# A prompt kernel whose mixer moves out of attention into a stage of its own

## The chip, the core and the metric

One core of a Trainium2 chip. The metric is the device time of one execution in microseconds, less is better. TensorE (PE) does matrix products, with its weight loads shown as PEld; VectorE (DVE), ScalarE (ACT) and GpSimd (POOL) do the rest; SyncE (SP), ACT and GpSimd issue DMAs, each through a queue that it works off in order.

## The reference

2048 tokens of width 576; 32 query heads on 16 key heads of width 128; attention sees the last 512 keys for every query, without a mask.

```
def _A_ref(x, k_cache, v_cache, wq, wo):
    W = min(4096, max(256, Sk // 4))
    q = (x @ wq).reshape(B, Sq, Hq, Dh), as heads
    k = jnp.repeat(k_cache[:, :, Sk - W:, :], rep, axis=1)
    v = jnp.repeat(v_cache[:, :, Sk - W:, :], rep, axis=1)
    p = _softmax(q k^T * (Dh ** -0.5))
    return (p v, heads side by side) @ wo

def _B_ref(x, w1, w2, w3, w4):
    h = _gelu(_layernorm(x, axis=-1) @ w1)
    c = D // 4
    g0, g1, g2, g3 = the four quarters of h, shifted along the tokens by +1, -1, +2, -2
    hs = jnp.concatenate([g0, g1, g2, g3], axis=-1) @ w2
    x1 = x + hs
    h2 = _gelu(_layernorm(x1, axis=-1) @ w3) @ w4
    return x1 + h2

x = A_x
xn = _layernorm(x, axis=-1)
s = _A_ref(xn, A_k_cache, A_v_cache, A_wq, A_wo)
g = _silu(_B_ref(xn, B_w1, B_w2, B_w3, B_w4))
return x + s * g
```

The products with w1 (576 x 576) and w2 (576 x 576), with the shift between them, are the mixer. Those with w3 (576 x 4608) and w4 are the MLP, which the text calls the up and the down product.

## The kernel before

The tokens are worked in 4 blocks of 512 (NB, QB), each of 4 tiles of 128 (TB). 576 is 4 chunks of 128 rows and one of 64 (NF = 4 full, NDC = 5), and on the output side 512 columns and 64 (M0, R0).

**Attention** runs over units u = 32 x block + head, 128 in all (U). A unit computes qT (`stage_q`), four score products with exp (`stage_s`), the value products (`stage_v`: 16 matmuls, a reciprocal and a product on DVE) and the transpose of the head's output into oT by a DMA on SP's queue (`stage_t`). The order of PE's, SP's and GpSimd's instructions is the program's. Other work is hung into the units by two tables: `at(u, fn)` for steps of any engine and `pe(u, atoms)` for matmuls, which are dealt out between the unit's own stages. The output projection of a block (`wo_atoms`: four groups of 32 matmuls of 512 columns, one for each tile, and a last group of 128 with 64 columns) goes into the first units of the next block; that of the last block follows after unit 127, one group after another. The mixer goes the same way: the second layernorm `ln2_steps`, its transposes `tr2`, the first product `b1` (five pieces a block, the last one the 64 remaining columns), its GELU out of tanh and DVE arithmetic (`gelu1`), the shift `b2_shift` of the remainder, and the second product `b2` and `b2_rem`, whose sum x1 goes to DRAM and is read back by `load_x1`.

**The flag.** `finish_flag` reduces the softmax's row sums, sends them through DRAM (`mx_dram`) onto one partition, and computes a flag that takes a safe path at the end where it is set. Its GpSimd part waits in `late`: a copy of one element of the first evicted projection tile into `gate`, ahead of the store.

**The MLP** starts when the last projection ends. Its products run as pairs of matmuls on 64 rows each, one on partitions 0 to 63 (LO) and one on 64 to 127 (HI), which work at the same time and write different banks. `up` does two chunks of 128 hidden columns in 9 such pairs: a first round, a DVE instruction that reads both banks (`fence`), and a second round with the halves crossed. `down` interleaves pairs of 512 and of 64 columns. Weights come in 9 slices (w3_s, w3r_s, w4_s; 4 + 0.5 + 4.5 KB a partition) by SP's queue into memory that attention has left; in the pools of this part each tile waits for the tiles that lay in its place (`reuse_waits="tile"`).

Of the kernel before, what the change touches and what calls it, by code (L numbers as in the profile page):

```python
# [31 lines left out]
def kernel(  # L32
# [45 lines left out]
    HW = OFF + QB + 4  # L78
    B1_ORDER = (4, 0, 1, 2, 3)
# [15 lines left out]
    x1_dram = dram.tile([S, D], BF16, name="x1_dram")  # L95
# [6 lines left out]
    def rsqrt_newton(pool, var, n):  # L102
# [5 lines left out]
        for _ in range(3):  # L108
# [3 lines left out]
            y2 = pool.tile([P, n], FP32, name="nr_y")  # L112
# [76 lines left out]
    xn_b = [keep.tile([P, TB, DP], BF16, name=f"xn_b{i}") for i in range(2)]  # L189
    xnn_b = keep.tile([P, TB, DP], BF16, name="xnn_b")  # L190
    x1_pool = ctx.enter_context(tc.tile_pool(name="x1_pool", bufs=2))
    small = ctx.enter_context(tc.tile_pool(name="small", bufs=4))
    x1_t = {}
    last_t = [None]
    xm_b = [xnn_b, xn_b[0]]
    g_last = xnn_b[:, 0, 0:D]

    def load_x1(b):
        x1 = x1_pool.tile([P, TB, D], BF16, name="x1")
        nc.sync.dma_start(out=x1[:], in_=rows(x1_dram, b * TB, TB))  # L200
        x1_t[b] = x1

    def ln3_steps(b):
        xm = xm_b[b % 2]
        dsts, srcs = [xm[:, tt, :] for tt in range(TB)], [x1_t[b][:, tt, :] for tt in range(TB)]
        return layernorm_small_steps(small, dsts, srcs) if b else layernorm_steps(small, dsts, srcs, twice=True)

    def ln3_transpose(b):
        for tt in range(TB):
            nc.sync.dma_start(out=xT_b[b % 2][:, :, tt * P:(tt + 1) * P], in_=xm_b[b % 2][:, tt, :], transpose=True)  # L210

    with ExitStack() as actx:
# [10 lines left out]
        xnnT = res.tile([P, NDC, QB], BF16, name="xnnT")  # L223
        w1_sb = res.tile([P, NDC, D], BF16, name="w1_sb")
        h4 = res.tile([P, TB, 4, 32], BF16, name="h4")
        w2_sb = res.tile([P, 5, D], BF16, name="w2_sb")
# [9 lines left out]
        hb_pool = pool("hb_pool", 2)  # L236
        hs_pool = pool("hs_pool", 1)
        g1_pool = pool("g1_pool", 1)
        oT_pool = pool("oT_pool", 36)
        wo_sb = pool("a_wo", 1).tile([P, Hq, D], BF16, name="wo_sb")  # L240
# [9 lines left out]
        def x_tile(b):  # L250
            if b < 2:
                xt = hb_pool.tile([P, 5, HW], BF16, name="hb")[:].rearrange("p a b -> p (a b)")
            else:
# [72 lines left out]
        for w in (xn_b[0], xnn_b):  # L326
            nc.gpsimd.memset(w[:, :, D:], 0.0)
# [1007 lines left out]
```

## Time and profile before

| | us |
|---|---|
| median of 3 runs | 821.14 (820.99 to 821.42) |
| span of the profiled execution, first to last instruction | 819.6 |
| PE busy | 810.0 |
| DVE, ACT, GpSimd busy | 467.2, 456.1, 96.4 |
| first matmul of the MLP | 534.85 after the span's start |

For the profiled execution the span is the time on record; the median of the runs lies 1.5 us above it. In a row of a view by line, the line is that of the source, then come the engine, the operation, output and inputs, the count, the busy time and the mean in ns of one, and the idle time in front of it with what ended it. A row of a view by stretches has the stretch, its length, busy time and count for PE, PEld, DVE, ACT and POOL, PE's granted clock, the share of time in which DMA engines were busy, and GB/s. A row of the order of time has start, duration, engine, line and operation. A row of the DMA issues ends with the size and the median us from issue to landing.

### The profile page before, as it was taken

How to read it: one execution, taken by the hardware profiler on the slowest of the kernel's cores; microseconds unless marked ns; L12 is line 12 of the kernel's file. 1: busy time of each engine (PE TensorE's matmuls, PEld its weight loads, DVE VectorE, ACT ScalarE, POOL GpSimd, SP SyncE). 2: the span in 40 equal slices, each digit the busy share in tenths (PEclk: the TensorE clock that was granted, in tenths of full speed). 3: DMA queues.
4: the chain of work that ended last, by engine and by line, in shares of the span. 5: the costliest groups of instructions: out<-in, count | busy, mean ns of one | idle time of the engine just before them, and what ended most of it. 6: DMA issues, size and time to landing. Idle time of an engine off the chain costs nothing. (4 is left out here: it accounts for less than half of the span.)

```text
span 819.6 us, 19524 instructions
## 1 busy us (share of the span) xinstructions
PE 810.0 (99%) x7945; PEld 469.1 (57%) x8031; DVE 467.2 (57%) x1447; ACT 456.1 (56%) x821; POOL 96.4 (12%) x164
## 2 busy tenths in 40 slices
PE   9999999999999999999999999999999999999998
PEld 6666655655564565565465655455555555555555
DVE  6878645678874357964346774044246636655413
ACT  7888853588783368994457983133332433334621
POOL 3443313010100110110001100000000000000000
PEclk9999999999999999999999999999999999999999
DMA  7998983364492144673035553994001221130101
GB/s 197 193 195 197 200 151 81 84 129 76 105 145 58 43 98 120 136 142 57 13 85 121 108 109 97 294 298 101 2 2 44 65 72 45 42 96 16 45 15 38
DMA packets 144156, 84.29 MB, mean 103 GB/s; under 512 B 110128, under 2 KB 136944, under 8 KB 144064
## 3 DMA queue, kind: packets, MB, share of 16 engines
q1 hardware_dynamic: 133408, 53.61, 32.1%
q0 software_dynamic: 9408, 28.15, 13.3%
q8 instruction: 63, 1.03, 0.5%
q10 hardware_dynamic: 1248, 1.25, 0.5%
q14 instruction: 29, 0.24, 0.1%
HBM read 49.17 MB, written 9.29 MB: 71 GB/s over the span
## 5 line engine op out<-in xcount | busy, mean ns | idle before, releaser
L496 ACT ACTIVATE pT<-sc 128x512 bf16<-128x512 f32 x512 | 285.5, 598 | 99.8 <-PE sc L492 90.4
L492 PE MATMUL sc<-qT,kT 128*128 128x512 bf16 x495 | 165.8, 379 | 0.2
L511 PEld LDWEIGHTS <-pT 128*128 128x128 bf16 x2048 | 134.3, 98 | 54.5 <-issue 11.0
L511 PE MATMUL po<-v_sb,pT 128*128 128x129 bf16 x2048 | 158.1, 220 | 0.9
L471 PE MATMUL psq<-xT_b,wq_b 128*128 128x512 bf16 x469 | 125.5, 379 | 1.9
L964 PE MATMUL ph<-xT_b,w_s 64*128 64x512 bf16 x976 | 127.3, 376 | 0.0
L1001 PE MATMUL pm<-w_s,h 64*128 64x512 bf16 x864 | 122.1, 377 | 0.0
L535 PE MATMUL pswo<-wo_sb,oT 128*128 128x512 bf16 x499 | 114.9, 379 | 0.6
L982 ACT ACTIVATE h<-ph 128x512 bf16<-128x512 f32 x67 | 39.4, 597 | 130.6 <-PE ph L964 128.4
L516 DVE TENSOR_TENSOR o<-po,ri_b 128x256 bf16<-128x256 f32 x256 | 107.9, 421 | 6.4 <-DVE ri_b L515 0.3
L1001 PEld LDWEIGHTS <-h 64*128 64x128 bf16 x1728 | 70.6, 94 | 55.4
L535 PEld LDWEIGHTS <-oT 128*128 128x128 bf16 x1024 | 65.2, 98 | 56.5
L1001 PE MATMUL pr<-w_s,h 64*128 64x64 bf16 x864 | 89.9, 189 | 0.0
L964 PEld LDWEIGHTS <-w_s 64*128 64x128 bf16 x1152 | 55.8, 94 | 48.2 <-issue 0.2
L471 PEld LDWEIGHTS <-wq_b 128*128 128x128 bf16 x506 | 49.4, 98 | 57.3 <-issue 1.0
L980 DVE COPY hx<-ph 128x512 f32<-128x512 f32 x55 | 38.1, 692 | 60.3 <-PE ph L964 60.3
L515 DVE RECIPROCAL ri_b<-po 128x2 f32<-128x2 f32 x256 | 42.2, 165 | 48.6 <-PE po L511 44.6
L492 PEld LDWEIGHTS <-kT 128*128 128x128 bf16 x512 | 46.8, 98 | 25.3 <-issue 0.2
L270 POOL DMA_DIRECT2D wq_b<-in_A_wq_dram x30 | 23.3, 776 | 303.8 <-PE sc L492 303.8
L479 DVE TENSOR_TENSOR qT<-psq,rq 128x512 bf16<-128x512 f32 x62 | 42.7, 689 | 27.0 <-ACT pT L496 20.3
L481 DVE CAST qT<-psq 128x512 bf16<-128x512 f32 x40 | 27.6, 689 | 32.9 <-PE psq L456 29.6
L982 ACT ACTIVATE h<-hx 128x512 bf16<-128x512 f32 x55 | 34.6, 630 | 6.0 <-DVE hx L980 1.7
(161 smaller groups left out, 722.7 us busy)
## 6 DMA issues: line engine op xcount, KB each, us to landing
wq_b<-in_A_wq_dram POOLq DMA_DIRECT2D x30, 512.0 KB, 5.1
wo_sb<-in_A_wo_dram POOLq DMA_DIRECT2D x8, 576.0 KB, 5.3
w_s<-in_B_w_dram SPq DMA_DIRECT2D x9, 512.0 KB, 6.8
w_s<-in_B_w_dram SPq DMA_DIRECT2D x10, 288.0 KB, 5.4
x_dram<-x SPq DMA_DIRECT2D x4, 576.0 KB, 4.1
x<-x_dram SPq DMA_DIRECT2D x4, 576.0 KB, 4.1
w_s<-in_B_w_dram SPq DMA_DIRECT2D x4, 576.0 KB, 8.3
s_b<-s_dram SPq DMA_DIRECT2D x4, 576.0 KB, 6.2
```

The lines of the kernel that those rows point to most:

```text
L471: nc.tensor.matmul(psq[:, :], lhsT=w[:, kc, hh * Dh:(hh + 1) * Dh], rhs=xT_b[qb % 2][:, kc, :], start=(kc == 0 and not (two and hh == 1)), ...
L479: behind["qT"] = nc.vector.tensor_tensor(out=qT[:, :], in0=psq[:, :], in1=rq_t.pop(u)[:, :], op=ALU.add)
L492: nc.tensor.matmul(sc[:, :], lhsT=kT[:, g, kc * P:(kc + 1) * P], rhs=qT_t[u][:, :], start=True, stop=True)
L496: behind["exp"] = nc.scalar.activation(out=pT[:, :], in_=sc[:, :], func=ACT.Exp, scale=SCALE)
L511: nc.tensor.matmul(po[:, j, :], lhsT=pTs[kc][:, tt * P:(tt + 1) * P], rhs=v_sb[:, g, kc, 0:Dh + 1], start=(kc == 0), stop=(kc == KCH - 1))
L515: nc.vector.reciprocal(out=ri, in_=po[:, :, Dh])
L516: nc.vector.tensor_tensor(out=o[:, t0:t0 + 2, :], in0=po[:, :, 0:Dh], in1=ri.unsqueeze(2).to_broadcast([P, 2, Dh]), op=ALU.mult)
L535: nc.tensor.matmul(ps, lhsT=oT_t[qb * Hq + h][:, tt, :], rhs=wo_sb[:, h, lo:hi], start=(h == 0), stop=(h == Hq - 1))
L964: nc.tensor.matmul(ps[i][:, :], lhsT=lhsT, rhs=xT[half, kc, :], start=first, stop=last, skip_group_check=True)
L980: nc.vector.tensor_copy(out=src[:, :], in_=ps[i][:, :])
L982: nc.scalar.activation(out=h3[:, :], in_=src[:, :], func=ACT.Gelu_apprx_tanh)
L1001: nc.tensor.matmul(out, lhsT=h3_t[b, fc][half, tt * P:(tt + 1) * P], rhs=w4_s[fc // WS][half, fc % WS, lo:hi], start=key not in started, s ...
```

## The change

The mixer's products, transposes, GELU and shift leave attention's tables. In attention stay the statistics of the second layernorm (`ln2_stats_steps`), and, in the last units, its application for blocks 0 and 1 (`ln2_apply`). xn is kept for all blocks, and x1 is formed in its place, so that `load_x1` and its DRAM copy go. Of the last block's projection, groups 0 and 1 begin within units 127 and 128; then comes the mixer of all four blocks; then groups 2, the small one and 3, and beside them the third layernorm of block 0.

In the stage, `chunk_pair` does two chunks of 512 columns as 9 pairs of 64-row matmuls with a fence between the rounds, as the MLP's `up` does, and `small_products` does the 64-column rest of a block as 18 pairs into two banks, which DVE adds. Each step's first round is issued ahead of the second round of the step before. GELU is one ACT instruction in place of tanh with DVE's arithmetic. The remainder of a block (`b1_rest`) is transposed by a DMA on SP's queue into hq; its shifted copy hs is written by DVE for 64 rows, from hq of the block and of the next one, and by a DMA on SP's queue for the other half. w1 and w2 are loaded at the stage's start by GpSimd's queue, behind `flag_rows`, into memory that attention held; xnnT of all blocks lies there too.

wo_sb, oT and the last projection's staging tile lie at the right edge of the memory. The MLP's weights take that place, `w3_s[0]` and `w3r_s[0]` lying just beside it, and are loaded by GpSimd's queue. In attention, the copies of qT that ACT did in blocks 1 to 3 are DVE's.

```diff
+    xn_b = [keep.tile([P, TB, DP], BF16, name=f"xn_b{i}") for i in range(NB)]
+    xm_b = [keep.tile([P, TB, DP], BF16, name=f"xm_b{i}") for i in range(2)]
+    ln2_mv = [keep.tile([P, TB, 2], FP32, name=f"ln2_mv{i}") for i in range(NB)]
+    ln2_r = [keep.tile([P, TB], FP32, name=f"ln2_r{i}") for i in range(NB)]
...
+    octx = ctx.enter_context(ExitStack())
+    so_last = octx.enter_context(tc.tile_pool(name="so_last", bufs=1, side="right")).tile([P, TB, D], BF16, name="so_last")
+    wo_sb = octx.enter_context(tc.tile_pool(name="a_wo", bufs=1, side="right")).tile([P, Hq, D], BF16, name="wo_sb")
+    oT_pool = octx.enter_context(tc.tile_pool(name="oT_pool", bufs=36, side="right"))
...
-                elif qb == 0 or hh == 0:
+                else:
                     nc.vector.tensor_copy(out=qT[:, :], in_=psq[:, :])
-                else:
-                    nc.scalar.activation(out=qT[:, :], in_=psq[:, :], func=ACT.Copy)
...
+        for b in range(2):
+            for tt in range(TB):
+                at(U - 6 + 2 * b + tt // 2, lambda b=b, tt=tt: ln2_apply(b, tt))
+        wo_last = wo_atoms(NB - 1)[0:2]
+        wo_last = wo_last[0][0:Hq - 1] + wo_last[1][0:8] + [wo_last[0][Hq - 1], flag_rows] + wo_last[1][8:]
+        pe(U - 1, wo_last[0:10])
+        pe(U, wo_last[10:22])
+        pe(U + 1, wo_last[22:])
...
-                c0, c1, c2 = (0, 2, n) if n == 5 else (0, n // 3, 2 * n // 3)
-                if u >= U - 2:
-                    c0, c1, c2 = (0, 5, 5) if u == U - 2 else (2, 4, 4)
+                c0, c1, c2 = (n // 2, n // 2, 3 * n // 4) if u == U else (0, n // 3, 2 * n // 3)
...
+        mctx = ExitStack()
+        mres = pool("m_res", 1, at=mctx)
+        xnnT = [mres.tile([P, NDC, QB], BF16, name=f"xnnT{b}") for b in range(NB)]
...
+        def chunk_pair(ps, lhs, rest_first):
+            n0, n1 = (NDC, NF) if rest_first else (NF, NDC)
+
+            def mm(i, half, k, first, last):
+                lhsT, rhs = lhs(i, half, k)
+                nc.tensor.matmul(ps[i][:, :], lhsT=lhsT, rhs=rhs, start=first, stop=last, skip_group_check=True)
+
+            def first():
+                for k in range(n0):
+                    for i, half in enumerate((LO, HI)):
+                        mm(i, half, k, k == 0, False)
+                fence(*ps)
+
+            def second():
+                for k in range(n1):
+                    for i, half in ((1, LO), (0, HI)):
+                        mm(i, half, k, False, k == n1 - 1)
+
+            return first, second
...
+        def small_products(ops):
+            pr = small_banks()
+            begun = set()
+            for t in range(0, TB, 2):
+                lo = [(t, k) for k in range(NDC)] + [(t + 1, k) for k in range(NF)]
+                hi = [(t, k) for k in range(NF)] + [(t + 1, k) for k in range(NDC)]
+                for both in zip(lo, hi):
+                    for j, (tt, k) in enumerate(both):
+                        lhsT, rhs = ops(HALVES[j], tt, k)
+                        out = pr[j][:, tt, :]
...
+                        nc.tensor.matmul(out, lhsT=lhsT, rhs=rhs, start=j not in begun,
+                                         stop=(tt == TB - 1 and both == (lo[-1], hi[-1])), skip_group_check=True)
...
+        def b1_rest(b):
+            def ops(half, tt, k):
+                w = w1_m[half, k, :].rearrange("p (g s) -> p g s", g=4)[:, :, P:c4] if k < NF else w1_q[half, :, :]
+                return xnnT[b][half, k, tt * P:(tt + 1) * P], w
+
+            pr = small_products(ops)
+            gs = gs_pool.tile([P, TB, R0], FP32, name="gs")
+            nc.vector.tensor_copy(out=gs[:], in_=pr[0])
+            nc.vector.tensor_tensor(out=gs[:], in0=gs[:], in1=pr[1], op=ALU.add)
+            nc.scalar.activation(out=h4[b % 2][:, :, 0:R0], in_=gs[:], func=ACT.Gelu_apprx_tanh)
+            nc.sync.dma_start(out=hq[:, OFF + b * QB:OFF + (b + 1) * QB].rearrange("p (t q) -> p t q", t=TB),
+                              in_=h4[b % 2][:].rearrange("p t c -> p (t c)"), transpose=True)
+
+        def shifts(b):
+            for g in (1, 0, 3, 2):
+                q = slice(32 * (g // 2), 32 * (g // 2) + (32 if g % 2 else rsz))
+                o0 = OFF + b * QB - SHIFT[g]
+                nc.vector.tensor_copy(out=hs[q, b * QB:(b + 1) * QB], in_=hq[q, o0:o0 + QB])
...
+        with tc.manual_schedule(engines={SP, POOL, PE, DVE, ACTE}):
+            nc.gpsimd.dma_start(out=w1_m[:], in_=B_w1[0:NF * P, :].rearrange("(kc p) m -> p kc m", p=P))
...
+            nc.gpsimd.dma_start(out=m1[:], in_=mx_dram[:, :].rearrange("(o p) c -> o c p", o=1))
+            for b in range(NB):
+                for tt in range(TB):
+                    if b >= 2:
+                        ln2_apply(b, tt)
+                    nc.sync.dma_start(out=xnnT[b][:, :, tt * P:(tt + 1) * P], in_=xm_b[b % 2][:, tt, :], transpose=True)
+
+            ops = [(b1_pair, 0), (b1_pair, 1), (b2_pair, 0), (b1_pair, 2), (b2_pair, 1), (b1_pair, 3), (b2_pair, 2),
+                   (b2_pair, 3)]
+            ops = [(f, b, p) for f, b in ops for p in range(2)]
+            aside = {0: [lambda: b1_rest(0)], 1: [lambda: b1_rest(1)], 2: [lambda: b1_rest(2)],
+                     3: [lambda: b1_rest(3), lambda: shifts(0)], 6: [lambda: shifts(1)], 8: [lambda: shifts(2)],
+                     10: [lambda: shifts(3)]}
+            pend = None
+            for k in range(len(ops) + 1):
+                nxt = None
+                if k < len(ops):
+                    f, b, p = ops[k]
+                    nxt = f(b, p, bank_pair((("pm0", "pm2"), ("pm1", "pm3"))[k % 3 - 1]) if k % 3 else h3_banks())
+                    nxt[0]()
+                for fn in aside.get(k, []):
+                    fn()
+                if pend:
+                    pend[1]()
+                    f, b, p = ops[k - 1]
+                    if f is b2_pair and p == 1:
+                        b2_rest(b)
+                pend = nxt
...
+            wo_b = wo_groups(NB - 1, wo_bank, None, nc.scalar)
+            for wo_i, i in enumerate((2, TB, 3)):
+                for atom in wo_b[i]:
+                    atom()
+            for step in ln3_steps(0):
+                step()
+            ln3_transpose(0)
+        mctx.close()
+        octx.close()
+
+        res = pool("b_res", 1, side="right")
...
         def load_w(i):
             c0 = i * WS * P
-            nc.sync.dma_start(out=w3_s[i][:, :, :],
+            nc.gpsimd.dma_start(out=w3_s[i][:, :, :],
                               in_=B_w3[0:NF * P, c0:c0 + WS * P].rearrange("(kc p) f -> p kc f", p=P))
...
-                nc.sync.dma_start(out=w4_s[i][:, k:k + n, :],
+                nc.gpsimd.dma_start(out=w4_s[i][:, k:k + n, :],
                                   in_=B_w4[c0 + k * P:c0 + (k + n) * P, :].rearrange("(fc p) d -> p fc d", p=P))
 
-        with tc.issue_after(last_t[0].ins):
-            for i in range(NSL):
-                load_w(i)
+        for i in range(NSL):
+            load_w(i)
```

456 lines of the change are left out of this document (180 added, 276 removed).

## The prediction

> **What bounds the kernel now.** I read the first part of the page, then stretches of the span by engine, then the groups of the mixer, then the order of time around the end of attention.
>
> ```profile
> PE 810.0 (99%) x7945; PEld 469.1 (57%) x8031; DVE 467.2 (57%) x1447; ACT 456.1 (56%) x821; POOL 96.4 (12%) x164
> ```
>
> ```profile
> 477.44:485.33 7.89, 7.84 (x73) 5.05 (x73) 5.99 (x20) 7.19 (x14) 0.00 (x0) 1.00 0.55 96
> 488.62:499.75 11.13, 11.03 (x87) 6.53 (x88) 6.82 (x17) 7.32 (x14) 0.00 (x0) 1.00 0.24 49
> 520.00:560.00 40.00, 39.95 (x485) 22.23 (x486) 13.99 (x53) 11.20 (x18) 1.10 (x1) 1.00 1.01 281
> 600.00:640.00 40.00, 40.00 (x516) 22.09 (x512) 23.32 (x71) 14.38 (x24) 0.00 (x0) 1.00 0.11 31
> ```
>
> ```profile
> 488.62:499.75 11.13, 4.26 (x15) 2.08 (x3) 1.00 0.24 49
> ```
>
> TensorE is busy 99% of the span, at granted clock 1.00 (third column from the right). That alone doesn't say that a matmul taken away shortens the kernel, so I compare two stretches of three heads each. Heads 120 to 122 hold nothing but attention: 7.89 us. Heads 124 to 126 hold the same and 15 matmuls of the mixer's second product (the row under them is that of the tile psx alone): 11.13 us. The difference, 3.24 us, is 0.216 a matmul: the full rate of a 512-column matmul as the output projection shows it (next rows). ACT is no fuller in the second stretch (7.32 against 7.19). So a matmul of the mixer in attention costs its whole time, and one taken out gives it back.
>
> ```profile
> 503.34 31.45 PEld L535 LDWEIGHTS <-oT 128*128 128x128 bf16 x256
> 503.61 27.57 PE L535 MATMUL pswo<-wo_sb,oT 128*128 128x512 bf16 x125
> 531.02 3.90 PE L535 MATMUL pswr<-wo_sb,oT 128*128 128x64 bf16 x128
> 534.85 1.04 PE L964 MATMUL ph<-xT_b,w_s 64*128 64x512 bf16 x8
> ```
>
> The last output projection is 128 matmuls of 512 columns (125 on record, 256 loads with the small ones) in 27.57 us: 0.2154 each. Its 128 of 64 columns run from 531.02 to 534.85: 0.030 each. The MLP follows without a gap.
>
> **What leaves attention.**
>
> ```profile
> L593 PEld LDWEIGHTS <-w_sb 128*128 128x128 bf16 x80 | 7.2, 98 | 6.1
> L603 PE MATMUL ph<-w_sb,xnnT 128*128 128x64 bf16 x80 | 3.3, 193 | 0.0
> L676 PEld LDWEIGHTS <-hb 128*128 128x128 bf16 x128 | 8.5, 98 | 2.5
> L676 PEld LDWEIGHTS <-hs 128*128 128x128 bf16 x32 | 3.1, 98 | 1.8
> L676 PE MATMUL psx1r<-w_sb,hb 128*128 128x64 bf16 x64 | 3.8, 193 | 0.1
> L676 PE MATMUL psx1r<-w_sb,hs 128*128 128x64 bf16 x16 | 2.7, 193 | 0.0
> ```
>
> By the loads, 80 + 80 wide products and 80 + 80 small ones: 160 x 0.2154 + 160 x 0.030 = 34.5 + 4.8 = 39.3 us out. The tanh on ACT and the GELU arithmetic on DVE that go with them, the x1 round trip through DRAM, and the qT copies moved from ACT to DVE lie beside PE and change nothing, as the two stretches show; if that cover failed, the plain heads at 7.89 us would not run at PE's rate with ACT busy 7.19.
>
> **What the new stage costs PE.** A pair of chunks has 9 slots of two 64-row matmuls in place of 10 matmuls, so 4 blocks x 2 products x 2 pairs x 9 = 144 slots, and as many pairs of 64-column matmuls. The slot's price is in the MLP, which runs such pairs: 100 matmuls a step (36 of the up product, 64 of the down, half of these small) are 34 wide slots and 16 small pairs. At 516 matmuls in 40.00 us a step takes 7.75; with 34 x 0.2154 = 7.32 the small pair is left with 0.027. So 144 x 0.2154 = 31.0. The small pairs stand alone here, in runs of 18, which no row shows: between 0.027 (hidden beside wide ones) and 0.060 (two at 0.030, one after the other), 3.9 to 8.6 us; I take 0.030, 4.3 us, as the MLP pair is the same instruction.
> The Trainium skill, "TensorE: Matmul & The Clock Gate", section "Back-to-back issue gap", says that start to start never falls below about 25 ns, however small the matmul: by it a pair would take 50 ns and the runs 7.2 us instead of 4.3. The trace speaks against it next to wide matmuls (0.027 for two); alone it isn't shown.
>
> ```profile
> L456 PEld LDWEIGHTS <-wq_b 64*128 64x128 bf16 x124 | 3.5, 94 | 13.1 <-issue 13.1
> ```
>
> The 128-row and 64-row kinds alternate twice more than before; at the change PEld stands still 13.1 us over 31 times, 0.42 each. Two are 0 to 0.8 us; I take 0.4. PE's own sum: -39.3 + 31.0 + 4.3 + 0.4 = -3.6 us.
>
> **What the stage waits for.** All four xnnT lie in memory that attention's K and V give back, and all 16 transposes stand in SP's queue behind the transpose of the last head; the mixer's own four (hq) stand behind these.
>
> ```profile
> 502.49 1.07 PE L511 MATMUL po<-v_sb,pT 128*128 128x129 bf16 x16
> 503.88 0.42 DVE L516 TENSOR_TENSOR o<-po,ri_b 128x256 bf16<-128x256 f32 x1
> 504.38 2.65 SPq L524 DMA_TRANSPOSE oT<-o  x1
> 479.42 5.24 SPq L210 DMA_TRANSPOSE xT_b<-xnn_b  x4
> xnnT<-xnn_b SPq DMA_TRANSPOSE x16, 2.7
> hb<-h SPq DMA_TRANSPOSE x4, 4.4
> L665 DVE COPY hs<-hb 32x512 bf16<-32x512 bf16 x16 | 4.5, 284 | 0.2
> hb<-in_A_x_dram SPq DMA_DIRECT2D x1, 72.0 KB, 2.2
> ```
>
> Let M be the time at which PE has done groups 0 and 1 of the projection and could begin the mixer. The head's last product ends 48 wide matmuls before M (M-10.3); in the trace its transpose is issued 0.77 after PE goes on to the projection (503.61 to 504.38), so at M-9.6. One transpose holds SP 1.31 (four in 5.24). xnnT starts at M-8.3, the 16 end at M+12.7, hq of blocks 0 and 1 are issued by M+14.0, and land 2.7 (as xnnT) to 4.4 later (as hb, which ran among weight loads); I take 3.5, M+17.5. The shifts of block 0, next on DVE, need both: four copies of 0.284, M+18.6; the copy of their half by SP lands 2.2 later (nearest row, a 72 KB load): M+20.8. The last slot of the second product's first pair reads it. PE gets there, waiting for nothing, after 48 slots and four runs of small pairs: 10.3 + 2.2 = M+12.5. So it waits 8.3 us in all up to there (7.5 to 9.2), split over the weights, b1_rest(3) (xnnT of block 3 lands at M-8.3 + 15 x 1.31 + 2.7 = M+14.1) and hs. Small pairs at 0.060 would put only the four later runs on the path, 2.2 us.
>
> ```profile
> 512.23 0.60 ACT L549 ACTIVATE hb<-pswo 128x512 bf16<-128x512 f32 x1 [9.74 <-PE pswo L535]
> 512.96 0.18 POOL L312 COPY gate<-hb 1x1 bf16<-1x1 bf16 x1 [38.61 <-ACT hb L549]
> 513.44 0.59 POOL L713 DMA_DIRECT2D mx_dram<-m  x1 [0.30 <-issue]
> L351 POOL DMA_DIRECT2D w_sb<-in_B_w_dram x1 | 0.8, 756 | 0.1
> L352 POOL DMA_DIRECT2D w_sb<-in_B_w_dram x1 | 0.5, 546 | 0.0
> w_sb<-in_B_w_dram POOLq DMA_DIRECT2D x1, 576.0 KB, 5.2
> w_sb<-in_B_w_dram POOLq DMA_DIRECT2D x1, 72.0 KB, 5.4
> ```
>
> GpSimd's queue has a wait too: the gate copy of flag_rows stands ahead of the w1 and w2 loads, and waits for ACT's copy of group 0, whose last matmul is 24 before M (M-5.2). From 512.23 to the end of the mx store are 1.8 us (and 0.2 from PE to ACT), so w1_m is issued at about M-3.2, the four small w1 loads up to M-0.3 (0.76 and four at 0.55), landing 5.2 to 5.4 later: M+2.0 to M+5.1. That is earlier than what SP brings and lies within the 8.3 us; behind the same copy stand w2 and all of the MLP's weights, which have time.
> On DVE the applies of blocks 2 and 3 stand ahead of the stage's first fence, and the last of them waits until block 1's transposes have read xm_b, M-8.3 + 7 x 1.31 + 2.7 = M+3.6, plus two applies (0.7). PE wants that fence after 10 slots and a run of small pairs, M+2.7: up to 1.6 us, also within the 8.3.
>
> ```profile
> L982 ACT ACTIVATE h<-pm 128x512 bf16<-128x512 f32 x22 | 11.9, 593 | 6.9 <-PE pm L964 6.9
> L982 ACT ACT_TABLE_LOAD x1 | 1.3, 1283 | 1.0 <-DMA w_s<-in_B_w_dram 1.0
> ```
>
> Behind hs, the second pair of blocks 1 and 2 reads the chunk whose GELU was only just begun: about 0.2, two at 0.59 and a semaphore, 1.4 us, against three slots (0.65) of cover: 0.8 each, 1.6 us (0 to 1.6). DVE's adds and copies then keep pace. The load of the GELU table, 1.28, moves from the MLP's start to this stage's and lies under PE's first gap; without one it would be under the first two pairs.
>
> **The MLP's start.** After the mixer PE has 64 wide and 128 small matmuls of the projection, 13.8 + 3.8 = 17.6 us.
>
> ```profile
> L154 DVE BATCH_NORM_STATS2 ln_st<-x 128x6 f32<-128x288 bf16 x24 | 10.6, 442 | 0.0
> L139 DVE TENSOR_SCALAR xnn_b<-xn_b,ln_mv,nr_y 128x576 bf16<-128x576 bf16 x16 | 6.3, 422 | 0.1
> wq_b<-in_A_wq_dram POOLq DMA_DIRECT2D x30, 512.0 KB, 5.1
> ```
>
> Under them DVE does the third layernorm of block 0 (8 x 0.44, 8 applies of at most 0.42, and some 15 small ones at about 0.2: 10 us) and SP its four transposes, 5.2 + 2.7 when one adds them: 17.9 at most, and they overlap. w3_s0 has room that nothing held, so it loads early. The rest of the MLP's weights takes oT's place, which the last group frees from its 17th matmul on, 3.2 us before the end: w4_s0, then w3_s1 at -2.4, landing 5.1 later at +2.7, where it's needed after 18 slots, at +3.9. A slice of 1.18 MB at 281 GB/s (the stretch 520 to 560) takes 4.2 us against 7.75 of PE. So 0, up to 1.5 us if the s and x loads of SP slow them.
>
> **Sum.** -3.6 + 8.3 + 1.6 = +6.3 us: 819.6 becomes 825.9 for the span, and the median of the runs lies 1.5 above the span (821.14), so 827.4. Its own range: down to 825 (hq in 2.7, no GELU waits), up to 833 (+0.9, +2.2, +0.4, +1.5).
>
> **Rivals.**
> The stage runs at PE's pace (faster). If transposes leave SP's queue early enough, at least a third faster than 1.31 each or ahead of the last head's, xnnT of block 3 is there before PE asks. It decides at 4 us of waits in all. With half of the GELU waits it is -3.6 + 0.8: 818.3; with w1's landing exposed (2 us) 820.3. For it: those transposes have SP nearly to themselves. Against: 1.31 is the pace in the row and the queue is in order. 0.17.
> The MLP's weights come late (slower still). If the whole of oT, not each buffer, has to be free, w4_s0 is issued when PE is done, w3_s1 0.8 after, and lands at +5.9 against +3.9, its small parts about 1.5 after that: +3.5 us, 831. For: GpSimd's queue is in order. Against: release is by tile. 0.12.
> The clock falls. At the entry PE may stand 2 to 5 us. No row here has such a gap and every clock in them is 1.00. At half rate for as long again as a gap of 3.5 us (the middle), PE would lose half of that, 1.7: 829. 0.08.
> The Trainium skill, "TensorE: Matmul & The Clock Gate", section "The HAM clock gate", has the clock halved after an idle window of about 3.4 us until as long a busy one; by that rule this rival needs the entry's wait in one piece, and I think it comes in two.
>
> **Chances.** The forecast holds 0.63, and the rivals as given. Under 0.2% (1.6 us, about what a measurement tells from no change) counts as the same: faster 0.13, same 0.06, slower 0.81. The range takes in the forecast, the rivals above it, and the rival below down to 819.5.
>
> **What would show it.** Right: heads with the mixer's work in the old kernel back at 7.89 us for three; PE with gaps at the mixer's first matmuls, before b1_rest(3) and before the matmul that reads hs, 7 to 9 us together; SP with 16 transposes in a row at 1.31; 9 slots a pair at 0.215; small runs of 18 in about 0.54. Wrong: gaps under 4 us in all, xnnT of block 3 landing before PE's third pair of chunks, runs of small pairs over 1 us, or a gap of PE at the MLP's first step.

## The result, and the profile after

The changed kernel took 845.8, 850.0, 883.4 and 885.0 us. Runs that were disturbed, here the two upper ones, are left out of every time and ratio in this document; of k_sx_only and i_early it is such a run that was profiled. With the two lower ones the ratio to the kernel before (821.25 us) is 1.0324, 95% interval 1.0298 to 1.0351. The forecast was 827.4 us, 819.5 to 833: the sign was right, the size was not. The profiled execution of the changed kernel took 849.96 us, its span 848.3; of the run of 845.8 us there is no trace. M is again the time at which TensorE has done groups 0 and 1 of the last projection.

First the busy time of PE, from the page, and stretches of the span by engine. The columns are PE, PEld, DVE, ACT and POOL busy, then granted clock, DMA share and GB/s.

```profile
PE 819.3 (97%) x8287; PEld 457.0 (54%) x8287; DVE 452.0 (53%) x1387; ACT 446.0 (53%) x797; POOL 124.9 (15%) x209
454.28:462.18 7.90, 7.90 (x75) 5.04 (x73) 5.43 (x15) 6.86 (x14) 0.00 (x0) 1.00 0.25 52
478.36:490.09 11.73, 0.01 (x2) 0.03 (x1) 2.04 (x7) 0.60 (x1) 4.82 (x14) 0.71 1.20 175
490.09:520.00 29.91, 20.84 (x243) 10.45 (x245) 9.51 (x28) 7.06 (x13) 3.61 (x9) 0.77 0.97 138
520.00:560.00 40.00, 39.18 (x521) 24.86 (x518) 26.23 (x81) 5.32 (x10) 1.78 (x3) 1.00 0.13 24
```

Heads 124 to 126, which held mixer work before and took 11.13 us, take 7.90: attention gave back what was forecast. Then PE stands still for 11.7 us, and is busy 20.84 of the next 29.91 us at a mean clock of 0.77. From 520 on it is full again. In order of time:

```profile
467.84 10.52 PE L234 MATMUL pswo<-wo_sb,oT 128*128 128x512 bf16 x48
490.09 1.89 PE L746 MATMUL ph<-xnnT,w_m 64*128 64x512 bf16 x8 [11.72 <-DMA xnnT<-xm_b]
519.71 0.59 PE L746 MATMUL pm<-w_q,hs 64*128 64x512 bf16 x2
544.30 7.08 PE L234 MATMUL pm<-wo_sb,oT 128*128 128x512 bf16 x32
561.95 1.04 PE L981 MATMUL ph<-xT_b,w_s 64*128 64x512 bf16 x8
```

The first row ends at M = 478.36. The first matmul that reads hs of block 0 is at 519.71, M+41.3, where the prediction had M+20.8. By the forecast's sum (35.7 us of PE and 9.9 of waits) the mixer ends at M+45.6, 24.8 us behind that matmul; 24.6 passed (544.30). So the lateness of 20.5 us comes wholly ahead of hs, and this is SP's queue in that time:

```profile
464.81 5.21 SPq L549 DMA_TRANSPOSE oT<-o  x2
472.40 0.37 SPq L950 DMA_DIRECT2D s_b<-s_dram  x1
472.94 0.39 SPq L952 DMA_DIRECT2D x_b<-in_A_x_dram  x1
473.38 33.54 SPq L871 DMA_TRANSPOSE xnnT<-xm_b  x16
506.96 0.58 SPq L950 DMA_DIRECT2D s_b<-s_dram  x1
507.96 1.20 SPq L808 DMA_TRANSPOSE hq<-h  x1
509.21 0.58 SPq L952 DMA_DIRECT2D x_b<-in_A_x_dram  x1
517.59 10.06 SPq L816 DMA_DIRECT2D hs<-hs  x3
```

Three things differ from the forecast. Two loads for the MLP, s and x of block 0, stand ahead of the transposes; s is issued only 2.4 us after the last head's transpose (SP waits 2.1 us for that to land), and the first transpose 3.3 us later than M-8.3. The 16 transposes take 33.54 us, 2.10 each on the mean instead of 1.31. And s and x of block 1 stand between the hq transposes. What was under way beside them, from the DMA issues between 470 and 520 (last number: median us to landing):

```profile
w_m<-in_B_w_dram POOLq DMA_DIRECT2D x2, 576.0 KB, 9.9
xnnT<-xm_b SPq DMA_TRANSPOSE x16, 8.4
```

The transposes landed 8.4 us after issue where 2.7 was taken, w1 and w2 9.9 instead of 5.2. The line of the transposes by itself shows how uneven they were (time on SP's queue in ns: least, median, most):

```profile
L871 SPq DMA_TRANSPOSE xnnT<-xm_b x16: 1213/1406/4327, 473.4 to 504.8; - x16
DMA to landing us min/median/max: 2.6/8.4/12.1
```

Half of them held SP for 1.41 us or less; three, of 4.06, 4.29 and 4.33 us, make up some 9 of the 12.6 us by which the 16 took longer than forecast. PE's waits between M and the MLP, and the largest of DVE's and ACT's that bear on hs:

```profile
PE ph L746 <- DMA xnnT<-xm_b: 11.7, 1, 11.7
PE pm L746 <- ACT hb L772: 5.0, 3, 4.1
PE pr L793 <- DMA xnnT<-xm_b: 2.2, 2, 1.7
PE pr L793 <- DVE gs L805: 1.8, 1, 1.8
DVE xm_b L207 <- DMA xnnT<-xm_b: 20.5, 6, 12.5
DVE hs L815 <- DMA hq<-h: 6.1, 1, 6.1
ACT h L807 <- DMA hq<-h: 13.7, 2, 11.9
```

The 4.1 us in PE's second row are one wait for a GELU of block 0 that stood on ACT behind the GELU of block 2's small products, which waited for h4's first buffer, that is for SP to get to hq of block 0.

### The profile page after: what moved, and what is told of

Read it like the earlier page. It is cut to its first block, busy times and chain, and to the rows that moved or that the text cites. A ratio compares the mean times of both kernels' runs of the same rounds, so it can differ in the third digit from the quotient of the medians.

```text
span 848.3 us, 20079 instructions
## 1 busy us (share of the span) xinstructions
PE 819.3 (97%) x8287; PEld 457.0 (54%) x8287; DVE 452.0 (53%) x1387; ACT 446.0 (53%) x797; POOL 124.9 (15%) x209
## 5 line engine op out<-in xcount | busy, mean ns | idle before, releaser
L517 PE MATMUL sc<-qT,kT 128*128 128x512 bf16 x512 | 171.6, 379 | 0.0
L498 PE MATMUL psq<-xT_b,wq_b 128*128 128x512 bf16 x506 | 129.8, 379 | 0.0
L981 PE MATMUL ph<-xT_b,w_s 64*128 64x512 bf16 x976 | 125.4, 376 | 0.1
L234 PE MATMUL pswo<-wo_sb,oT 128*128 128x512 bf16 x448 | 103.2, 379 | 0.0
L1018 PEld LDWEIGHTS <-h 64*128 64x128 bf16 x1728 | 62.1, 94 | 64.0
L508 DVE CAST qT<-psq 128x512 bf16<-128x512 f32 x64 | 44.1, 689 | 77.4 <-PE psq L483 46.3
L1018 PE MATMUL pr<-w_s,h 64*128 64x64 bf16 x864 | 83.1, 189 | 0.0
L981 PEld LDWEIGHTS <-w_s 64*128 64x128 bf16 x1152 | 48.6, 94 | 56.0 <-DMA w_s<-in_B_w_dram 0.6
L488 ACT ACTIVATE rq<-sc 128x512 f32<-128x512 f32 x62 | 33.6, 595 | 8.0 <-PE sc L483 8.0
```

The costliest lines, as they stand in the source:

```text
L234: nc.tensor.matmul(ps, lhsT=oT_t[qb * Hq + h][:, tt, :], rhs=wo_sb[:, h, lo:hi], start=(h == 0), stop=(h == Hq - 1))
L498: nc.tensor.matmul(psq[:, :], lhsT=w[:, kc, hh * Dh:(hh + 1) * Dh], rhs=xT_b[qb % 2][:, kc, :], start=(kc == 0 and not (two and hh == 1)), ...
L508: nc.vector.tensor_copy(out=qT[:, :], in_=psq[:, :])
L517: nc.tensor.matmul(sc[:, :], lhsT=kT[:, g, kc * P:(kc + 1) * P], rhs=qT_t[u][:, :], start=True, stop=True)
L981: nc.tensor.matmul(ps[i][:, :], lhsT=lhsT, rhs=xT[half, kc, :], start=first, stop=last, skip_group_check=True)
L1018: nc.tensor.matmul(out, lhsT=h3_t[b, fc][half, tt * P:(tt + 1) * P], rhs=w4_s[fc // WS][half, fc % WS, lo:hi], start=key not in started, s ...
```

## The experiments

Each kernel ran beside the kernel before on the same chip (medians of 820.8 to 821.1 us). The times from M are worked out from each timeline; the ratio is that to the kernel before.

| run | ratio (95%) | 16 transposes | hs read | MLP begins |
|---|---|---|---|---|
| forecast | 1.0076 | 20.96 us | M+20.8 | M+63.2 |
| changed kernel | 1.0324 (1.0298–1.0351) | 33.54 | M+41.3 | M+83.6 |
| a_sx_late | 1.0308 (1.0273–1.0343) | 31.99 | M+33.3 | M+75.6 |
| b_sx_late_w_early | 1.0169 (1.0154–1.0183) | 22.37 | M+23.8 | M+66.2 |
| c_warm | 1.0376 (1.0361–1.0391) | 32.81 | M+43.2 | M+85.8 |
| d_h4_four | 1.0150 (1.0134–1.0166) | 23.62 | M+23.3 | M+65.6 |
| e_sx_in_mlp | 1.0118 (1.0096–1.0140) | 22.75 | M+21.7 | M+64.7 |
| f_xm_four | 1.0172 (1.0122–1.0222) | 23.4 | M+22.2 | M+65.1 |
| g_proj_ahead | 1.0162 (1.0144–1.0181) | 32.26 | M+31.6 | M+69.2 |
| h_weights_on_sp | 1.0161 (1.0139–1.0183) | 23.80 | M+23.6 | M+66.3 |
| k_sx_only | 1.0211 (1.0168–1.0253) | 23.44 | M+27.1 | M+69.3 |
| m_sx_by_gpsimd | 1.0194 (1.0164–1.0224) | 25.23 | M+26.4 | M+68.7 |
| i_early | 1.0104 (1.0089–1.0119) | ten left | – | – |
| j_reordered | 1.0080 (1.0065–1.0094) | ten left | M+18.4 | M+55.4 |
| l_held | 0.9979 (0.9968–0.9989) | ten left | M+16.9 | M+53.7 |

**a_sx_late.** The loads of s and x go behind the third layernorm's transposes.

```diff
-        load_sx(0)
+        with tc.issue_after(ln3_dma[0].ins):   # last transpose of ln3_transpose(0)
+            load_sx(0)
...
-                load_sx(b + 1)
+                with tc.issue_after(ln3_dma[0].ins):
+                    load_sx(b + 1)
```

> Edit: the MLP's loads of s and x for blocks 0 and 1 (1.15 MB each) are issued behind the third layernorm's transposes, and no longer among the mixer's transposes on SP's queue. Loads theory: in the changed kernel the transposes start 3.3 us late because s stands ahead of them and waits for the last head's transpose, and go at 2.1 us each instead of 1.31 because the loads of s, x, w1 and w2 share the DMA engines with them. Without s and x they start at M-8, the first gap of PE falls from 11.7 to about 5 us (w1 landing at about M+5), the pitch lies between 1.31 and 2.1 (w1, w2 and the first MLP slice still load), and hs of block 0 is issued some 12 us earlier: about 838 us. Queue theory (16 transposes in a row go at 2.1 us each by themselves, whatever else loads): only the 3.3 us and the two issues between hq come back, 5.5 us: about 844. Clock theory (the lost time is PE at half clock behind the long gap): with a first gap of 5 us the clock still falls, and more than half of the loss stays: 840 or more, with granted clock under 0.8 from M+5 to M+30.

The transposes start at M-8.3 and hs comes 8.0 us earlier, but their pace hardly changes. SP's row:

```profile
469.98 31.99 SPq L873 DMA_TRANSPOSE xnnT<-xm_b  x16
```

So s and x cost their place in the queue (3.3 us ahead, and the rest between hq and behind it), not the pace. Of the 8.0 us the profiled span kept 6.5 (841.8 against 848.3), since s and x now ran beside the MLP's first weights: PE waited 1.9 us for a slice. The times alone settle nothing: a's ratio isn't told from that of the changed kernel (the intervals overlap), and its 843.4 us in the profiled execution lies nearest to the 844 of the queue theory. The next run decides.

**b_sx_late_w_early.** Also w1 and w2 out of the way, loaded 24 and 20 heads before the end.

```diff
+    w_pool = octx.enter_context(tc.tile_pool(name="w_pool", bufs=1, side="right"))   # w1_m, w1_p, w1_q, w2_q
+    w2_m = ...   # in xT_b[0]
...
+        at(U - 24, lambda: late(pT_t[U - 24][0][0:1, 0:1], load_w1))
+        at(U - 20, lambda: late(pT_t[U - 20][0][0:1, 0:1], load_w2))
```

> Edit: as a_sx_late, and w1 and w2 are loaded some 20 heads before the end of attention, into free memory and into the x tile that attention has done with, so that no large load runs beside the transposes. Loads theory: 16 transposes at 1.31 us each from M-8, landing 2.7 us after issue, no wait for w1; what is left is the chain that the prediction summed (last transpose at M+13, hs of block 0 issued at about M+19 to M+21): 827 to 829 us. Queue theory: the pitch stays at about 2.1, the last transpose is issued at M+25 and hs at M+32: 839 or more. Clock theory: PE's waits come in pieces of up to 4 us, the clock dips below 0.8 for 10 us or more: 832 or more even with transposes at 1.31.

```profile
470.06 22.37 SPq L880 DMA_TRANSPOSE xnnT<-xm_b  x16
```

1.40 each: the row from the kernel before very nearly holds for 16 in a row when nothing else loads, and the queue theory falls. (The MLP's first slice left this stretch too; it is issued only at 527.27.) hs is read at M+23.8, 3.0 us later than forecast. The time, 834.3 us, is still 5 over what was expected; e finds most of it. By its time alone the clock theory (832 or more) isn't excluded here; c speaks against it.

**k_sx_only and m_sx_by_gpsimd** complete the comparison: s and x of block 0 alone beside the transposes, once on SP's queue and once on GpSimd's.

```diff
+            load_sx(0)        # ahead of the transposes; k: nc.sync, m: nc.gpsimd
             for b in range(NB):
                 for tt in range(TB):
```

> Edit: as b_sx_late_w_early, with the loads of s and x for block 0 (1.15 MB) put back where the changed kernel has them, on SP's queue ahead of the 16 transposes; w1 and w2 stay early. With the runs before, it makes the four cases of the two sets of loads: both beside the transposes (the changed kernel, 2.10 us a transpose), w1 and w2 alone (a_sx_late, 2.00), neither (b_sx_late_w_early, 1.40). Bytes theory (any load of that size slows the transposes alike): 1.7 us or more each, and 838 to 845 us. Weights theory (the loads of w1 and w2 on GpSimd's queue do it, s and x do little): at most 1.5 us each on the mean, 834 to 837.

> Edit: as k_sx_only, with the same loads of s and x for block 0 (1.15 MB) issued by GpSimd in place of SP, and so after GpSimd's store of the row range, at about M-3, as w1 and w2 in a_sx_late; nothing else loads beside the transposes. Queue theory: loads on GpSimd's queue slow SP's transposes where loads on SP's own do not: the mean rises from 1.47 us (k_sx_only) to 1.6 or more while s and x load, and 837 us or more. Shape theory (w1 and w2 slow the transposes by their many small rows, or by their 0.5 MB more, not by their queue): 1.40 to 1.50 us each, 832 to 835 (SP starts its transposes 1 us earlier than in k_sx_only).

SP's row of k, whose profiled execution reached this stretch 24 us later, so that only its length is read:

```profile
495.95 23.44 SPq L891 DMA_TRANSPOSE xnnT<-xm_b  x16
```

And of m:

```profile
470.35 25.23 SPq L892 DMA_TRANSPOSE xnnT<-xm_b  x16
```

Without any load beside them, the 16 transposes took 22.37 to 23.80 us (b, d, e, f and h in the table). k's 23.44, with 1.15 MB on SP's own queue, lies among these. m's 25.23, with the same 1.15 MB on GpSimd's queue, is 1.4 to 2.9 us more, and the 31.99 and 32.26 of a and g, with w1, w2 and the first MLP slice on GpSimd's queue (1.95 MB), are 8.2 to 9.9 more. The bytes theory (1.7 us or more each) is refuted by both k and m. That the queue makes a difference rests on one trace each, m's 1.58 a transpose being just short of the 1.6 expected, and it isn't the whole of it: at 1.4 to 2.9 us for 1.15 MB, 1.95 MB would cost 2.4 to 4.9. Whether the rest is due to the many short rows of w1's and w2's remainders wasn't tried. In time, m took 836.9 us and k between 835.1 and 843.8, too wide a spread to tell them apart. The Trainium skill, "DMA: Bandwidth & Descriptors", section "SWDGE vs HWDGE vs iDMA", says that loads issued by GpSimd and by SP feed different internal queues of the same DMA engines, which take them in turn. The trace agrees as far as m's 1.4 to 2.9 us go; that this taking in turn is what delays the transposes is argued, not shown.

**c_warm.** The entry gap filled with matmuls that nothing reads.

```diff
+            wu = ps_h2.tile([P, QB], FP32, name="pm1")
+            for _ in range(54):
+                nc.tensor.matmul(wu[:, :], lhsT=wo_sb[:, 0, 0:P], rhs=wo_sb[:, 0, 0:QB], start=True, stop=True)
             ops = [(b1_pair, 0), (b1_pair, 1), (b2_pair, 0), ...
```

> Edit: the changed kernel with 54 matmuls of 128 rows by 512 columns (11.6 us of PE) put ahead of the mixer's first product, into a bank that nothing reads; the wait of 11.7 us for the first transposes is filled and nothing else is moved. Loads theory: hs of block 0 is set by SP's chain, which doesn't know of PE's clock, so the granted clock is near 1.00 at the mixer's first pairs and the time stays within 2 us of the changed kernel's (848 to 850 against 850). Clock theory: with the clock kept up the pairs behind the gap run at 0.215 a slot instead of up to 0.43, and 6 us or more come back (844 or less).

```profile
478.00:490.00 12.00, 12.00 (x57) 5.32 (x55) 1.28 (x4) 0.60 (x1) 3.25 (x6) 1.00 1.16 108
510.00:520.00 10.00, 4.38 (x23) 1.68 (x22) 1.34 (x5) 2.99 (x7) 0.00 (x0) 0.66 0.73 116
PE ph L746 <- DMA w_q<-in_B_w_dram: 3.7, 1, 3.7
```

The first two rows are stretches, the third is from PE's waits. The clock stayed at 1.00 through the old gap, and nothing came back: 850.8 to 852.5 us against 845.8 and 850.0. The gap isn't filled without a rest, as PE then stood 3.7 us for a part of w1 that came later than in the changed kernel. But SP's chain doesn't know of it: hq of block 0 is issued at 507.89 and the copy into hs at 517.71, against 507.96 and 517.59. The waits only moved: 6.7 us in one piece for the GELU behind hq, in a stretch of mean clock 0.66. So in this stage the half clock behind the first gap is a companion of the waits, not a cost on top of them.

**d_h4_four.** On top of b, h4 gets four buffers.

```diff
-        h4 = [mres.tile([P, TB, P], BF16, name=f"h4_{i}") for i in range(2)]
+        h4 = [mres.tile([P, TB, P], BF16, name=f"h4_{i}") for i in range(NB)]
```

> Edit: as b_sx_late_w_early, with four h4 buffers in place of two, so that ACT's GELU of the small products of blocks 2 and 3 no longer waits for SP to have transposed those of blocks 0 and 1 (in the changed kernel it waited 11.9 us, with the GELUs of block 0's second pair and of block 1 behind it). Chain theory (SP's order of transposes alone sets when hs comes): 0 to 1 us less than b_sx_late_w_early. ACT theory (the two buffers are a wait of their own in ACT's order): 3 us or more less.

833.2 against 834.3 us: 1.1 less, so ACT's wait for hq was mostly in the shadow of SP's order.

**e_sx_in_mlp.** On top of d, s and x still later.

```diff
-        load_sx(0)
-        work = ln3_work(1)
+        work = ln3_work(1) + [lambda: late_sx(0)]      # behind ln3_transpose(1) on SP
```

> Edit: as d_h4_four, with the loads of s and x for blocks 0 and 1 held back further, behind the third layernorm's transposes of block 1, some 30 us into the MLP. In b_sx_late_w_early and d_h4_four those loads ran beside the first MLP slices: PE waited 1.5 us for a slice, and from its first matmul to the end of the span the MLP took 287.9 and 288.1 us, against 284.8 in the kernel before. Loads theory: that difference goes: about 285 us for the MLP, 830 in all. Rival (the MLP is slower for a reason of its own, such as the weights' queue or x1 kept in SBUF): 833.

830.4 us, as expected: no wait for a slice, and the MLP took 286.0 us. The 1.3 us that remain against the kernel before lie behind the last instruction of DVE (3.5 us to the end of the span instead of 2.2); 1.0 of them is the last store, 24 KB, which landed in 2.4 us instead of 1.4. In the changed kernel it took 2.6. Why, wasn't tried.

**f_xm_four.** On top of e, the second layernorm of blocks 2 and 3 gets tiles of its own.

```diff
+        for b in range(2, NB):
+            xm_m[b] = mres.tile([P, TB, DP], BF16, name=f"xm_m{b}")
```

> Edit: as e_sx_in_mlp, and the second layernorm of blocks 2 and 3 is applied into two tiles of their own, so that DVE needn't wait until SP has transposed blocks 0 and 1. In b_sx_late_w_early PE waited 4.7 us in one piece for DVE, whose first fence and first copies stand behind those applies, and the granted clock fell to 0.58. Chain theory (SP's 16 transposes, hq and hs alone set the stage): PE's wait moves from the entry to hs of block 0, which is issued at M+21 as before: 0 to 1 us less than e_sx_in_mlp. DVE theory (this wait and the half clock behind it are on the path): 3 us or more less.

The wait for DVE is gone (4.5 us in e), its place taken by 2.9 and 1.3 us for xnnT, and hs is read at M+22.2 against M+21.7. The runs took 831.3 to 838.1 us, the lowest against 830.0 in e: no gain. The chain theory stands.

**h_weights_on_sp.** On top of e, load_w issues by nc.sync behind ln3_transpose(0).

```diff
-            nc.gpsimd.dma_start(out=w3_s[i][:, :, :],
+            nc.sync.dma_start(out=w3_s[i][:, :, :],      # and w3r_s, w4_s
```

> Edit: as e_sx_in_mlp, with the MLP's weights back on SP's queue, behind the third layernorm's transposes of block 0. Loads theory: GpSimd's queue has no part in the loss: within 2 us of e_sx_in_mlp (a little slower, since the first slice is issued later). Rival (queue theory of GpSimd: its weight loads are dearer to issue or to land and hold the MLP back): 2 us or more faster than e_sx_in_mlp.

834.8 us, 4.4 slower than e, more than either expectation allowed; PE waited 2.1 us for slices at the MLP's start and the MLP took 289.1. That GpSimd's queue holds the MLP's weights is no part of the loss; it is worth some 3 us in the MLP. The rest arose ahead of it (M+66.3 against M+64.7) and isn't explained.

**g_proj_ahead.** Two projection groups as cover, w1 and w2 as in the change.

```diff
+            for wo_i, i in list(enumerate((2, TB, 3)))[:2]:
+                for atom in wo_b[i]:
+                    atom()
             ops = [(b1_pair, 0), (b1_pair, 1), (b2_pair, 0), ...
```

> Edit: the changed kernel with group 2 and the small group of the last output projection put ahead of the mixer (10.7 us of PE), the third layernorm of block 0 spread over the mixer's later pairs, four h4 buffers, and s and x loaded some 30 us into the MLP; w1 and w2 stay where they are. Chain theory: the mixer begins at M+10.7, its chain (last xnnT at M+15 to M+17, hs of block 0 at M+21 to M+23) is covered but for a few tenths, and what is left of the waits are the GELU waits of 1.6 us: 820 to 822 us, no more than 1 us from the kernel before. Rival (w1 and w2, still loaded beside the transposes, keep their pitch at 1.7 to 2.1, so that the chain ends at M+30): 827 or more.

The rival was right. With s and x gone, w1, w2 and the first slice alone keep the pace at 2.02:

```profile
470.04 32.26 SPq L873 DMA_TRANSPOSE xnnT<-xm_b  x16
```

834.4 us: 10.7 us of cover don't reach where the chain is 10 us longer, and the layernorm spread over the last pairs made DVE late there (PE waited 4 us for it).

**i_early, j_reordered, l_held.** What the reasons above ask for: fewer transposes behind the last head, no large load beside them, products in an order that never wants what is just being made.

```diff
+        for tt in range(TB):
+            at(U - 12 + 2 * tt, lambda tt=tt: ln2_transpose(0, tt))     # into xT_b[0]
+        for tt in range(2):
+            at(U - 2 + tt, lambda tt=tt: ln2_transpose(1, tt))          # into xT_b[1]
...
-            ops = [(b1_pair, 0), (b1_pair, 1), (b2_pair, 0), (b1_pair, 2), (b2_pair, 1), (b1_pair, 3), (b2_pair, 2),
+            ops = [(b1_pair, 0), (b1_pair, 1), (b1_pair, 2), (b2_pair, 0), (b1_pair, 3), (b2_pair, 1), (b2_pair, 2),   # j, l
...
+                        with tc.issue_after(last_o[0].ins):             # l: behind attention's last o
                             ln2_apply(b, tt)
```

> Edit: as e_sx_in_mlp, but six of the 16 transposes (block 0 and half of block 1) are issued between the last twelve heads of attention, into the two x tiles that attention has done with; w2 waits in attention's third staging buffer instead. Ten transposes are left behind the last head's. Chain theory: they end at M+5, hq of blocks 0 and 1 follow at once, hs of block 0 is issued at M+11 to M+12, so PE never waits over 1 us in one piece and the clock stays at 1.00. Sum: PE's own part of the change -3.6, the runs of small pairs at about 0.66 each as measured in the traces of the changed kernel (8 x 0.12 over the prediction: +1.0), GELU waits 1.2 to 1.6, hs and xnnT 0.5 to 1.5, and 1.2 that all changed kernels spend after their last instruction: 820 to 821.5 for the span, 821.5 to 823 us. Rival (the six early transposes hold up the last heads' own on SP's queue, and PE waits in the projection): 825 or more.

> Edit: as i_early, with the first product of block 2 put ahead of the second product of block 0 and that of block 3 ahead of the second product of block 1, and the shifts of block 0 ahead of the small products of block 3. No second product then reads a GELU that was only just begun, and hs of block 0 is wanted 4 us later. Chain theory: the waits for GELU and for hs go, 1.2 to 2.5 us less than i_early: 820 to 821.5, level with the kernel before. Rival (DVE, which has 5.1 us of work for every 4.5 us of PE in a block of the second product, sets the pace at the end, where three such blocks now stand behind one another): no gain or up to 2 us slower than i_early.

> Edit: as j_reordered, with the second layernorm of blocks 2 and 3 held on DVE behind attention's last normalization, and the shifts of block 0 behind the small products of block 3 again. In j_reordered four of those applies stood between attention's own instructions on DVE (they wait for block 0's transposes, which now run early), and attention ended 5.4 us later than in e_sx_in_mlp, while the stage itself took 55.5 us from M to the MLP against 64.6. Held back, attention ends as in e_sx_in_mlp, the stage stays at 55.5 less the one wait of 1.5 us for ACT: 533 + 286 = 819 to 820 us for the span, 820.5 to 822 us: level with the kernel before. Rival (attention was held up by the early transposes on SP's queue, not by DVE): no change, 826 to 828.

i took 829.0 us and j 827.4, each some 6 us over the range expected. In j's trace the stage had become as short as forecast (M+55.4), but M itself was 5.4 us late (483.6). PE's longest wait in attention, from its waits between 440 and 485:

```profile
PE sc L525 <- DVE qT L516: 2.7, 1, 2.7
```

It ends at 445.71. What DVE did just ahead of that copy of qT:

```profile
444.42 0.64 DVE L209 TENSOR_SCALAR xm_b<-xn_b,ln_mv,ln_r 128x576 bf16<-128x576 bf16 x2 [4.26 <-DMA xT_b<-xm_b]
```

An apply for block 2 stood ahead of attention's own work on DVE, which stood 4.26 us for a transpose of block 0. Behind PE's wait the clock was at half for 3.4 us (last section), in which PE lost some 1.7 us by estimate; with a second wait of 0.5 us these are 4.9 of the 5.4. Neither expectation had the applies in it. Held back in l, they no longer stand there, and M is 478.5. The end of the projection's groups 0 and 1 and the MLP's begin in l_held, in order of time:

```profile
467.96 10.52 PE L243 MATMUL pswo<-wo_sb,oT 128*128 128x512 bf16 x48
532.17 1.04 PE L1002 MATMUL ph<-xT_b,w_s 64*128 64x512 bf16 x8
```

And the stretch between M and 520 by engine:

```profile
478.00:520.00 42.00, 41.72 (x605) 23.42 (x603) 27.35 (x79) 11.89 (x22) 3.09 (x4) 1.00 0.38 55
```

PE is busy 41.72 of 42 us at clock 1.00, and the MLP begins at M+53.7: less 17.6 of projection and 0.3 of waits, the mixer took 35.8 us of PE, against 31.0 + 4.3 + 0.4 = 35.7 forecast. l_held takes 819.2 us against 821.1, ratio 0.9979 (0.9968 to 0.9989): faster than the kernel before by a bare 0.2%, and than the changed one by 3%.

## Why the prediction failed, step by step

**What leaves attention: right.** Three heads take 7.90 us, forecast 7.89; M came at 478.36, and 517.2 (that of the kernel before, 64 wide and 128 small matmuls ahead of its 534.85) less 39.3 is 477.9.

**What the stage costs PE: right.** 35.8 against 35.7 us, in l_held. A run of small pairs with nothing beside it, in b, between the first of its rows and the wide matmul behind it:

```profile
479.78 0.30 PE L815 MATMUL pr<-w_m,xnnT 64*128 64x64 bf16 x8
480.31 1.04 PE L768 MATMUL pm<-xnnT,w_m 64*128 64x512 bf16 x8
```

It took 0.53 us (forecast 0.54); those of the second product took 0.64. The Trainium skill, "TensorE: Matmul & The Clock Gate", section "Back-to-back issue gap", would have 0.9 by its floor of 25 ns; 36 matmuls in 0.53 us are 15 ns each, so for pairs of 64-row matmuls the trace speaks against it here too.

**What the stage waits for: the step that failed.** Two sentences of it: "xnnT starts at M-8.3" and "One transpose holds SP 1.31", taken from four transposes with SP to themselves and used for 16 beside loads that the prediction itself placed there (w1 issued at M-3.2). Measured, xnnT started at M-5.0 and a transpose held SP 2.10 on the mean. The delay of SP's loads of s and x was priced only at the MLP's start ("up to 1.5 us"); that they would stand ahead of the transposes was not seen, as they aren't in the order written by hand. The 20.5 us come out of the traces so, to within 0.1: 3.3 for s and x ahead; 12.6 for the pace (33.54 less 20.96), of which a, g and the runs without loads put some 8 to 10 on w1, w2 and the first slice, while 1.4 to 2.8 are there without any load; 1.7 for s and x of block 1 between the hq transposes; 2.5 for the landing of hq of block 1 (the first shift at 515.89, issued at 509.91: 6.0 instead of 3.5), with x just ahead of it on the queue; 0.5 for the shifts and their copy. Taken away (e), hs is read at M+21.7, 0.9 from the forecast: the chain was the right one and the sizes were wrong.

The span missed by 22.4 us (848.3 against 825.9). The other 1.9 are 0.4 at M, 1.6 in the MLP (most of it behind the last instruction of DVE, as in e), and -0.1 of rests.

**GELU waits: right in the sum.** Behind hs, three of 0.4 to 0.5 us, 1.3 in all, where two of 0.8 were forecast. **DVE's applies: mis-sized.** PE waits 4.7 us for them in b where the forecast had up to 1.6; that cost nothing, as it lies within the chain's time (f).

**The MLP's start: right** for the changed kernel, where no wait appears. The rival of late weights assumed that all of oT must be free first, and that did not show. With s and x moved next to them (a, b, d) 1.5 to 1.9 us did appear, the size that the forecast gave that collision.

**Rivals.** The stage at PE's pace was given 818.3 to 820.3, "if transposes leave SP's queue early enough [...] or ahead of the last head's": l_held does that, at 819.2, with several edits more. The change did not. The clock did fall, and PE's wait at the entry came in one piece, not the two that were expected; but the price of it as an addition, 1.7 us, was nothing in this stage (c). In j, where PE sets the time, a half clock of 3.4 us cost about that much.

**The range** ended at 833 because every term of the wait was bounded by rows of the kernel before, the lightest or the median ones. Rows that spoke against it were there: hq "ran among weight loads" at 4.4 us instead of 2.7, and by their line (28 transposes in all; the landing is that of all 28) single ones had held SP for 2.7 us and landed after 9.3:

```profile
L406 SPq DMA_TRANSPOSE xnnT<-xnn_b x16: 1201/1272/2749, 106.8 to 356.0; - x16
DMA to landing us min/median/max: 2.6/3.3/9.3
```

## What to carry to other kernels

A transpose's pace read from four of them alone says little about 16 beside loads: list what every queue has under way in that stretch, and bound the pace by a row with traffic, its longest and not its median. Before moving a stage behind a chain of transfers, ask which loads of the next stage are free to be scheduled into its queue ahead of it, and tie them down. A wait that is filled or taken away off that chain (c, d, f) comes back elsewhere.

## What the runs showed of the hardware

In these traces the granted clock is full or half, never between but where a stretch holds the change. Of the changed kernel, in stretches of 1 us (the clock is the third number from the right):

```profile
482.00:483.00 1.00, 0.00 (x0) 0.00 (x0) 0.44 (x2) 0.00 (x0) 0.33 (x1) 1.00 0.85 272
483.00:484.00 1.00, 0.00 (x0) 0.00 (x0) 0.00 (x0) 0.00 (x0) 0.00 (x0) 0.65 1.33 165
484.00:485.00 1.00, 0.00 (x0) 0.00 (x0) 0.22 (x1) 0.00 (x0) 0.74 (x2) 0.50 1.31 149
493.00:494.00 1.00, 1.00 (x21) 0.54 (x17) 0.00 (x0) 0.00 (x0) 0.70 (x2) 0.73 0.05 5
494.00:495.00 1.00, 0.60 (x6) 0.19 (x3) 0.64 (x2) 0.00 (x0) 0.00 (x0) 1.00 1.30 96
497.00:498.00 1.00, 1.00 (x37) 0.88 (x34) 0.04 (x1) 1.00 (x1) 0.00 (x0) 0.50 2.12 164
```

PE's gaps ahead of the last of these, in brackets:

```profile
496.35 0.19 PE L793 MATMUL pr<-w_m,xnnT 64*128 64x64 bf16 x1 [1.75 <-DVE gs L805]
496.87 0.32 PE L793 MATMUL pr<-w_m,xnnT 64*128 64x64 bf16 x7 [0.34 <-DVE gs L806]
```

PE stops at 478.36; the clock is at 0.50 from 483.3 on, 5.0 us later, and back at 493.5, 3.4 us after PE's return at 490.09. The Trainium skill, "TensorE: Matmul & The Clock Gate", section "The HAM clock gate", has a free-running window of about 3.4 us, idle or busy; 5.0 and 3.4 us fit that. Less than a window without work was enough, though: the clock was at 0.50 again from 497.0, although PE had been idle since its return only for gaps of 1.75 and 0.34 us. And in j one gap of 2.73 us, up to 445.71, was enough:

```profile
446.00:447.00 1.00, 0.91 (x3) 0.34 (x3) 0.69 (x3) 0.60 (x1) 0.00 (x0) 0.55 0.00 0
447.00:448.00 1.00, 1.00 (x4) 0.40 (x3) 0.28 (x1) 0.00 (x0) 0.00 (x0) 0.50 0.07 19
449.00:450.00 1.00, 1.00 (x10) 0.71 (x9) 0.59 (x2) 0.56 (x1) 0.00 (x0) 0.74 0.28 48
```

The clock is at 0.50 from 446.1 to 449.5, while PE is busy.

An undisturbed transpose is steady: between 1.30 and 1.33 us from one to the next in 13 of the 15 steps of b.
